# Features of six query groups turned by DMA as two 16-bit planes instead of by TensorE

## The chip, the cores and the metric

The kernel runs on one core of one Trainium2 chip. The metric is the time of one execution in microseconds of device time; smaller is better. A profiled execution also gives a span (from its first to its last recorded instruction) and a trace of every engine: PE (TensorE), DVE (VectorE), ACT (ScalarE), POOL (GpSimd) and SP, whose queue issues nearly all of this kernel's DMAs.

## The reference

Two stages stand behind each other. The first is attention with polynomial features: for each of 4 batches and 4 heads, with 1088 positions and 32 values a head, each row of q and k is projected with S1 and with S2 to 8 values each, and the outer product of the two gives 64 features. The second is a feed-forward layer with a squared ReLU, 128 to 2048 to 128, on all 4352 tokens.

```python
def phi(x):
    a = np.einsum('rd,bhsd->bhsr', S1, x)
    b = np.einsum('rd,bhsd->bhsr', S2, x)
    return np.einsum('bhsi,bhsj->bhsij', a, b).reshape(*x.shape[:-1], r * r)
q_p, k_p = (phi(q), phi(k))
kv = np.einsum('bhsf,bhsd->bhfd', k_p, v)
z = np.sum(k_p, axis=2)
num = np.einsum('bhsf,bhfd->bhsd', q_p, kv)
den = np.einsum('bhsf,bhf->bhs', q_p, z)[..., None] + 1e-06
x = (num / den), heads side by side          # 4352 x 128
out = relu(x @ w_in) ** 2 @ w_out
```

The output is 4352 x 128 in float32.

## The kernel before

**Tiling.** A batch's 1088 positions are 1024, dealt as eight positions to each of 128 partitions, and a remainder of 64. The 1024 are worked as two groups of four tiles of 128 tokens: group (b, g) is half g of batch b, 512 tokens with all four heads. The remainders of two batches share a tile.

**What is done to a group of q.** `turned` (L247, DVE) or, for groups (0, 1) and (3, 1), `proj_t` (L230, PE) brings the 32 values of a head onto partitions. `projected` (L210, PE) projects with S1 and S2, `features` copies the result out of PSUM (L59, ACT) and forms the outer products `ph` (L251, POOL in most groups): 128 tokens by 1024 values, that is 4 tiles with 256 features (4 heads of 64). The features have to lie on partitions for the next product, so `feature_t` (L390) turns them with PE, eight transposes of 128x128 in float32 into two PSUM tiles, and ACT copies each to SBUF (L59, `sb`). `numerators` (L210, `nd`) multiplies them with the batch's k-v sums `kvbd`. `normalize` (L443 to L482, DVE and two small steps of POOL) divides by the denominator and scales each token into 16 bits; the scale is kept in `beta` and multiplied back at the store. Its result `xs` is turned by a DMA transpose from SP (L486) into `xT`, except in three chunks where PE does it.

**What is done to a group of k.** `k_gen` turns, projects and forms features in the same way, and sums them with v (`Kv`, L313, PE). The sums are copied to `kvbd` by DVE (L60). Numerators of batch b need the sums of batch b. From batch 2 on, v is loaded by 32 small DMAs (`load_v`, L110).

**The feed-forward stage** runs over chunks of 512 tokens, one for each group of q (group (0, 0) gives two chunks of 256, and all remainders give one of 256). A chunk is 16 blocks. A block is a first product (`pg`, L708, 16-bit operands, 512 wide), its ReLU (ACT, L715, `gt`), the square (DVE, L716, `g2`) and the second product (`po`, L735, float32), which sums over the 16 blocks in PSUM. `first_product` and `block` keep the first product LOOK = 2 blocks ahead of the second. `pg` has two PSUM buffers, `g2` three SBUF buffers. At the end of a chunk ACT copies the sum (L648), PE turns it back (L652), DVE scales it (L681) and SP stores it (L689). The last chunk (L745) is computed with tokens on partitions already.

**Order.** The first part, up to the first group, is written out by hand (`start`). Behind it the program is recorded in lanes: each generator yields how many blocks are to pass before its next piece, `pump` runs at most two pieces between two blocks, and `drain` empties the lanes. A planner in the compiler then orders each engine's instructions by its own expectation of when operands are ready; what stands in `pinned` stays behind all that was recorded before it on its engine, and so do the loads marked pin and the DMA transposes on SP. At run time every engine and the SP queue work strictly in the order they were given. In batch b the lanes of the first half hold group (b, 1) of q, all of k for batch b+1 and the remainders; those of the second half hold group (b+1, 0) of q. The loads of k and v for batch b+2 are recorded ahead of a batch (ahead of the second half for b = 0) and q's ahead of the second half.

**PSUM and SBUF tiles that the change touches.** `t_ps` shares the two PSUM buffers tagged "ms" with other small tiles; `nd` and the k-v sums share one buffer tagged "nd". `phT0` and `phT1` have two SBUF buffers each.

## Time and profile before

| | |
|---|---|
| median of 3 runs | 210.41 us (210.34 to 210.86) |
| the profiled execution | 210.01 us |
| its span | 208.1 us |
| PE busy | 198.9 us |
| DVE busy | 146.5 us |
| ACT busy | 108.6 us |
| POOL busy | 46.2 us |
| granted TensorE clock | 1.00 |
| bytes moved by DMA | 12.15 MB |

How to read it: the page gives the busy time of each engine, the chain of work that ended last (followed back from the last instruction, at each step to what released it), and groups of instructions by line with the number of times, the busy time in all, the mean time of one in ns, and the idle time of the engine just before them with what ended it. A busy PE is not a PE at its peak, since matmuls are pipelined. Idle time of an engine that is not on the chain costs nothing. Rows of a timeline give start, length, engine, line, operation, destination and source, the number of merged instructions, and in brackets how long the engine stood idle before and who released it.

### The profile page before, as it was taken

What the parts mean: (1) busy time and instruction counts of PE and PEld (TensorE: products, weight loads), DVE (VectorE), ACT (ScalarE), POOL (GpSimd) and SP (SyncE); (2) the same over time, 40 slices, a digit from 0 to 9 for tenths busy, and PEclk for the clock granted to TensorE, in tenths of its full rate; (3) what the DMA queues carried; (4) which work ended last, traced back from release to release, by engine and by line L of the source; (5) the groups of instructions that cost most, each with busy time, mean ns of one, the idle gap of its engine ahead of it and who ended that gap; (6) DMA issues with size and microseconds to landing.
All of it is one profiled execution on the core that took longest, in us unless ns stands there. A gap on an engine that the chain in (4) does not pass through costs nothing.

```text
span 208.1 us, 5407 instructions
## 1 busy us (share of the span) xinstructions
PE 198.9 (96%) x2217; PEld 123.9 (60%) x2217; DVE 146.5 (70%) x281; ACT 108.6 (52%) x206; POOL 46.2 (22%) x66
## 2 busy tenths in 40 slices
PE   7979997999999999999999999999999899999993
PEld 6857885754535553555534556446445454779992
DVE  2869569657787899767776667666968677766662
ACT  3458673265455546356455553555555445555550
POOL 1001346004040863004220951031103110000000
PEclk9999999999999999999999999999999999999999
DMA  6899205222324121402010201010000101010001
GB/s 167 220 339 323 43 3 143 36 31 52 103 67 99 31 35 54 129 1 54 0 27 5 52 3 28 0 36 18 11 14 16 37 3 25 2 50 13 16 0 50
DMA packets 29000, 12.15 MB, mean 58 GB/s; under 512 B 16560, under 2 KB 28592, under 8 KB 28976
## 3 DMA queue, kind: packets, MB, share of 16 engines
q1 hardware_dynamic: 28896, 11.81, 21.8%
q8 instruction: 17, 0.28, 0.6%
q14 instruction: 7, 0.06, 0.1%
q10 hardware_dynamic: 80, 0.01, 0.0%
HBM read 8.79 MB, written 2.23 MB: 53 GB/s over the span
## 4 chain that ended last, share of the span: by engine, by line
PE 88%; DVE 7%; POOL 2%; issue 1%; ACT 1%; DVEq 0%; ACTq 0%
PE po L735 47%; PE pg L708 14%; PE po L745 7%; PE nd L210 4%; PE ab_ps L210 4%; PE t_ps L390 3%; DVE g L716 3%; PE kv_ps L313 3%; PE o_ps L652 2%; PE kv_first L189 1%; PE xt_ps L230 1%; POOL ph L251 1%; PE kv_first L313 1%; DVE xs L473 1%; DVE rtop L453 1%
## 5 line engine op out<-in xcount | busy, mean ns | idle before, releaser
L716 DVE TENSOR_TENSOR g<-gt 128x512 f32<-128x512 f32 x136 | 102.2, 762 | 44.3 <-ACT gt L715 42.7
L735 PE MATMUL po<-g,w_o 128*128 128x512 f32 (+1 forms) x288 | 123.3, 525 | 1.2 <-DVE g L716 1.2
L715 ACT ACTIVATE gt<-pg 128x512 f32<-128x512 f32 x136 | 81.3, 600 | 53.7 <-PE pg L708 52.1
L735 PEld LDWEIGHTS po<-g,w_o 128*128 128x128 f32 x288 | 52.3, 191 | 27.6 <-issue 11.1
L251 POOL TENSOR_TENSOR ph<-ab 128x512 f32<-128x512 f32 (+1 forms) x27 | 31.9, 1204 | 64.8 <-ACT ab L59 64.8
L708 PE MATMUL pg<-xT,w_in 128*128 128x512 f16 x112 | 42.6, 381 | 0.0
L708 PEld LDWEIGHTS <-w_in 128*128 128x128 f16 x160 | 15.3, 98 | 20.4 <-issue 16.8
L479 POOL TENSOR_SCALAR mp<-mm 128x4 f32<-128x4 f32 (+2 forms) x11 | 5.8, 527 | 54.2 <-DVE mm L459 54.2
L745 PEld LDWEIGHTS po<-w_o,g 128*128 128x128 f32 x128 | 16.6, 192 | 0.6
L745 PE MATMUL po<-w_o,g 128*128 128x128 f32 x128 | 16.6, 276 | 0.0
L59 ACT COPY sb<-t_ps 128x512 f32<-128x512 f32 (+1 forms) x18 | 9.2, 515 | 10.4 <-PE t_ps L390 10.4
L59 ACT COPY ab<-ab_ps 128x256 f32<-128x256 f32 (+1 forms) x19 | 6.4, 340 | 15.7 <-PE ab_ps L210 14.1
L210 PEld LDWEIGHTS ab_ps<-w_bd,xt 128*32 128x32 f32 (+1 forms) x476 | 8.9, 114 | 6.9 <-issue 4.2
L210 PE MATMUL ab_ps<-w_bd,xt 128*32 128x64 f32 (+1 forms) x476 | 11.9, 223 | 0.4 <-DVE w_bd L774 0.3
L390 PEld LDWEIGHTS t_ps<-iden,ph 128*128 128x128 f32 x60 | 7.5, 141 | 6.8 <-issue 4.9
L210 PEld LDWEIGHTS nd<-kvbd,sb 128*32 128x32 f32 x480 | 7.9, 110 | 5.4 <-issue 2.6
L210 PE MATMUL nd<-kvbd,sb 128*32 128x66 f32 x480 | 9.6, 222 | 0.0
L390 PE MATMUL t_ps<-iden,ph 128*128 128x128 f32 x60 | 9.4, 274 | 0.0
L59 ACT COPY xt<-xt_ps 128x512 f32<-128x512 f32 (+1 forms) x11 | 5.1, 471 | 5.5 <-PE xt_ps L230 5.4
L708 PE MATMUL pg<-xT_h,w_in 128*128 128x256 f16 x32 | 6.1, 274 | 0.0
L313 PEld LDWEIGHTS kv_ps<-v_main,ph 128*32 128x32 f32 x384 | 3.9, 109 | 3.7 <-POOL beta L482 1.7
L247 DVE STREAM_TRANSPOSE xt<-t 128x512 f32<-128x512 f32 x9 | 6.1, 693 | 0.0
(71 smaller groups left out, 110.5 us busy)
## 6 DMA issues: line engine op xcount, KB each, us to landing
t<-in_k_dram SPq DMA_DIRECT2D x3, 512.0 KB, 3.9
t<-in_q_dram SPq DMA_DIRECT2D x3, 512.0 KB, 4.4
out_dram<-o_sb SPq DMA_DIRECT2D x20, 64.0 KB, 1.7
w_in<-in_moe_w_in_dram SPq DMA_DIRECT2D x2, 512.0 KB, 6.7
w_o<-in_moe_w_out_dram SPq DMA_DIRECT2D x2, 512.0 KB, 7.7
v_turned<-in_v_dram SPq DMA_DIRECT2D x64, 16.0 KB, 1.7
k_sb<-in_k_dram SPq DMA_DIRECT2D x2, 256.0 KB, 3.0
q_sb<-in_q_dram SPq DMA_DIRECT2D x2, 256.0 KB, 4.8
```

Of the source, the lines that this page charges most:

```text
L59: return nc.scalar.copy(dst, src)
L210: nc.tensor.matmul(out_ps[p0 + c : p0 + c + m, c0 : c0 + w], lhsT[:, l0 + c : l0 + c + m], rhs,)
L247: nc.vector.transpose(out=xt[:, :], in_=_v(src, 128 * g, [[NJ * D, 4], [1, 128]]))
L251: eng.tensor_tensor(out=_v(ph, 256 * t0, [[64, 4 * w], [8, 8], [1, 8]]), in0=_v(ab, 64 * t0, [[16, 4 * w], [1, 8], [0, 8]]), in1=_v(ab, 64 ...
L313: nc.tensor.matmul(self.ps[c : c + self.m, at : at + w], _v(ph, c0 + 128 * pr + c, [[1, self.m]], p0, n), v_of(2 * pr + c // 64), start=c ...
L390: nc.tensor.transpose(t_ps[:, 128 * t : 128 * t + 128], ph[:, 256 * t + 128 * pr : 256 * t + 128 * pr + 128], iden[:, :],)
L479: nc.gpsimd.tensor_scalar(out=mp[:, 0:T], in0=mm[:, 0:T], scalar1=1.0 / 1024.0, scalar2=None, op0=mult)
L708: nc.tensor.matmul(pg[:, nt * i : nt * i + nt], w_in[:, 128 * (c + i) : 128 * (c + i) + 128], xT[:, 0:nt],)
L715: last_relu[0] = nc.scalar.activation(gt[:, :], pg[:, :], Relu).ins
L716: nc.vector.tensor_tensor(out=g2[:, :], in0=gt[:, :], in1=gt[:, :], op=mult)
L735: last_product[0] = nc.tensor.matmul(po[0][:, 0:nt], w_o[:, 128 * c : 128 * c + 128], g2[:, nt * i : nt * i + nt], start=(c == 0), stop=(c ...
L745: nc.tensor.matmul(po[t // 2][:, 128 * (t % 2) : 128 * (t % 2) + 128], g2[:, 128 * t : 128 * t + 128], w_o[:, 128 * c : 128 * c + 128], st ...
```

## The change

For the six groups of batches 1 to 3 the features are no longer turned by PE. `features_by_dma` sees the float32 features as pairs of 16-bit halves. ACT copies the low halves into one tile of 128x1024 16-bit elements and the high halves into another (`cut`, four copies of 128x512). SP turns each tile with one DMA transpose into eight blocks of 128x128 (`plane`). ACT then writes the two planes into the low and high halves of `phT` (four copies of 128x512, every second 16-bit element written). The two transposes are pinned in SP's order.

The work is recorded earlier, too. What made a group from turn to numerators in one lane (`q_gen`) is cut in two: `phi_gen` (turn, projection, features, planes) and `x_gen` (numerators, normalization). `phi_gen` of (b+1, 0) and then its `x_gen` are recorded in the first half of batch b, that of (b+1, 1) in the second half of batch b, and `x_gen` of (b, 1) in the first half of batch b. `x_gen` waits in its lane until the batch's k-v sums are done (`summed`), and for (3, 1) until nine chunks exist. The `drain` in the middle of a batch is gone. Group (0, 1) keeps PE's transposes (`second_gen`).

Last, LOOK is 3, and `g2` has four buffers.

```diff
+    def features_by_dma(ph, eng):
+        cut = [apool.tile([128, 1024], U16, name=f"cut{x}", tag=f"cut{x}") for x in range(2)]
+        turned = [apool.tile([128, 1024], U16, name=f"plane{x}", tag=f"plane{x}") for x in range(2)]
+        halves = ph.bitcast(U16)
+        for x in range(2):
+            for y in range(2):
+                eng.copy(
+                    cut[x][:, 512 * y : 512 * y + 512], _v(halves, 1024 * y + x, [[2, 512]])
+                )
+            pinned(nc.sync.dma_start_transpose(
+                _v(turned[x], 0, [[128, 8], [1, 128]]), cut[x][:, :]
+            ))
+            yield 1
+        yield 4
+        phT = [
+            apool.tile([128, 512], F32, name=f"phT_d{pr}", tag=f"phT{pr}") for pr in range(2)
+        ]
+        for x in range(2):
+            for pr in range(2):
+                eng.copy(
+                    _v(phT[pr].bitcast(U16), x, [[256, 4], [2, 128]]),
+                    _v(turned[x], 128 * pr, [[256, 4], [1, 128]]),
+                )
+                yield 1
+            yield 1
+        return phT
...
-    def x_gen(b, g, phT, m=32):
+    def x_gen(b, g, phT=None, m=32):
+        while b not in summed or (b, g) == (B - 1, 1) and len(chunks) < LAST:
+            yield 1
+        if phT is None:
+            phT = phT_of[b, g]
         nd = numerators(b, phT, m)
...
-    def q_gen(b, g, outer, m=32):
+    def phi_gen(b, g, outer):
         eng = nc.scalar
-        if (b, g) == (0, 1):
-            ph = features(ab_second[0], 4, "ph_q", eng, outer)
-        else:
-            xt = proj_t(q_sb[b], g, 4, eng) if (b, g) in BY_PE else turned(q_sb[b], g)
-            yield 1
-            ph = proj(xt, 4, "ph_q", eng, outer, m=m)
+        xt = proj_t(q_sb[b], g, 4, eng) if (b, g) in BY_PE else turned(q_sb[b], g)
+        yield 1
+        ph = proj(xt, 4, "ph_q", eng, outer)
+        yield 3
+        phT_of[b, g] = yield from features_by_dma(ph, eng)
+
+    def second_gen(outer, m):
+        ph = features(ab_second[0], 4, "ph_q", nc.scalar, outer)
         yield 3
         phT = []
         for pr in range(2):
-            phT.append(feature_t(ph, 4, pr, eng))
+            phT.append(feature_t(ph, 4, pr, nc.scalar))
             yield 1
-        yield from x_gen(b, g, phT)
+        yield from x_gen(0, 1, phT)
...
-    LOOK = 2
+    LOOK = 3
...
-        g2 = fpool.tile([128, 512], F32, tag="g2")
+        g2 = fpool.tile([128, 512], F32, tag="g2", bufs=4)
...
-        add_work(second if b == 0 else q_gen(b, 1, (pool,)))
+        add_work(second if b == 0 else x_gen(b, 1))
         if b + 1 < B:
             add_work(k_gen(b + 1, (pool,)), after=6 if b == 0 else 0)
+        if b + 1 < B:
+            add_work(
+                phi_gen(b + 1, 0, (pool,)), x_gen(b + 1, 0), after=7 if b == 0 else 2
+            )
...
-        drain()
...
         if b + 1 < B:
-            add_work(q_gen(b + 1, 0, (pool,)))
+            add_work(phi_gen(b + 1, 1, (pool,)))
```

In the changed file the parting copies are L409, their transposes L412, the joining copies L422, DVE's turn L248, the ReLU L755, the square L756, the second product L775 and the transpose of `xs` L517.

## The prediction

> **What bounds the kernel now.** I read the page first (engine shares, chain that ended last, costliest groups), then the busy time by stretch, then the SP queue in order of time, then one stretch of the timeline. Groups are named (batch, group); an output chunk is 512 tokens of one group.
>
> ```profile
> span 208.1 us, 5407 instructions
> PE 198.9 (96%) x2217; PEld 123.9 (60%) x2217; DVE 146.5 (70%) x281; ACT 108.6 (52%) x206; POOL 46.2 (22%) x66
> ...
> PE 88%; DVE 7%; POOL 2%; issue 1%; ACT 1%; DVEq 0%; ACTq 0%
> ...
> L59 ACT COPY sb<-t_ps 128x512 f32<-128x512 f32 (+1 forms) x18 | 9.2, 515 | 10.4 <-PE t_ps L390 10.4
> ...
> L390 PE MATMUL t_ps<-iden,ph 128*128 128x128 f32 x60 | 9.4, 274 | 0.0
> ```
> PE carries the end; ACT has room in sum. In the chain in order of time a block (second product 0.86, next first product 0.21) repeats every 1.075 us, and four feature transposes (L390) take 0.44.
>
> The busy time by stretch, cut where a chunk's store begins on PE, the first at a chunk's start (length, then busy of PE, PEld, DVE, ACT, POOL):
> ```profile
> 45.00:66.80 21.80, 21.80 (x144) 10.41 (x141) 15.76 (x28) 11.73 (x21) 5.15 (x6) 1.00 0.31 78
> 66.80:91.95 25.15, 24.70 (x384) 13.18 (x383) 21.39 (x41) 12.68 (x25) 9.42 (x11) 1.00 0.23 53
> 91.95:112.46 20.51, 20.51 (x159) 10.17 (x157) 15.23 (x26) 11.29 (x20) 4.89 (x6) 1.00 0.08 21
> 112.46:137.10 24.64, 24.64 (x386) 13.48 (x384) 16.09 (x30) 12.70 (x26) 9.56 (x9) 1.00 0.07 18
> ```
> Sixteen blocks are 17.2 us. With the other PE work of each stretch, by the chain's durations (store transposes 0.44, projections 0.58 a group, numerators 1.07, k-v sums 1.75, feature transposes 0.87), the work is 22.2, 20.2 and 23.4 us in the last three: PE stood still for 2.9, 0.3 and 1.2 us, and by the same count 0.7 and 1.4 in the next two. The reader sees PE busy all the time; the gaps are in the waits. The second stretch shows their cause:
> ```profile
> 68.39 5.04 POOL L251 TENSOR_TENSOR ph<-ab 128x512 f32<-128x512 f32 x4 [8.74 <-ACT ab L59]
> ...
> 71.15 1.35 DVE L716 TENSOR_TENSOR g<-gt 128x512 f32<-128x512 f32 x1
> ...
> 72.42 1.02 DVE L453 TENSOR_TENSOR rtop<-small,small 128x4 f32<-128x4 f32 x1
> ...
> 75.33 1.13 PE L735 MATMUL po<-g,w_o 128*128 128x512 f32 x2 [0.41 <-DVE g L716]
> ```
> While POOL makes features, DVE's squares take 1.2 to 1.5 us instead of 0.69, and PE waits for squares. The SP queue:
> ```profile
> 32.44 0.38 SPq L79 DMA_DIRECT2D t<-in_k_dram  x1
> 32.88 16.94 SPq L110 DMA_DIRECT2D v_turned<-in_v_dram  x32
> 49.91 0.39 SPq L79 DMA_DIRECT2D t<-in_q_dram  x1
> ...
> 60.55 16.59 SPq L110 DMA_DIRECT2D v_turned<-in_v_dram  x32
> ...
> 83.43 1.22 SPq L486 DMA_TRANSPOSE xT<-xs  x1
> ```
> SP is a queue with two plugs of 17 us: the 32 small loads of v. What stands behind one starts late.
>
> **Removed from PE.** Eight transposes a group, 2 x 0.44; six groups: 5.2 us. On ACT 12 copies of 0.585 go (7.0 us). Projections, numerators and the DVE turn stay and only move.
>
> **Added on ACT.** 48 copies of 128x512 16-bit elements, every second one read or written. No row shows such a copy; nearest is the cast from SBUF to 16 bits (L795), 0.635 us, two of which start 0.50 apart when nothing is waited for. Ends: 0.48 apart, as ACT's copies from PSUM follow each other, and 1.0 if skipping halves the rate. I take 0.5, the nearest row. ACT's busy time becomes 108.6 - 7.0 + 48 x 0.6 = 130 us; a ReLU and one copy fit in a block (1.0 of 1.075). What counts is the order: parting waits for POOL, joining for a DMA, and ReLUs stand behind both. With two pg buffers a ReLU has two blocks less its own time, 2.15 - 0.21 - 0.60 - 0.06 = 1.3 us, before PE stops; LOOK = 3 leaves that as it is and gives squares one block (1.075) more.
>
> **Added on SP.** Twelve transposes of 128x1024. The row is half as wide: 1.19 us of SP, landing 2.3 us after issue begins. Ends: 1.2 us if issue is fixed, 2.4 if it doubles. Plain loads of any width cost SP about 0.4, so I take a fixed 0.4 and 0.8 for each 512 columns: 2.0, landing at 3.2. By the Trainium skill (Advanced Engine Details and Errata, X-Bar Transpose) transposing DMAs are as fast as regular ones; by that rule the sum would be the last one under cheap transposes. The row of 1.19 beside 0.38 for a load of four times the bytes contradicts it here.
>
> **The walk down the queues**, in the changed program's instruction order with the durations above.
> - Batch 1's first group. POOL's features of q stand behind one k group and ahead of the other: 28.2 + 2 x 2.54 = 33.3. The four parting copies end at 33.9 and 34.9, with ReLU 14 of the first chunks and the other k group's copy behind them; that group's features end at 37.8 instead of 34.9, still ahead of the PSUM buffer that its sums need (freed by the normalization of (0,1) at 38.9). From there 1.5 of k-v sums, 2.15 of second products and 0.4 of small work bring PE to chunk (0,1) at 43.1, its first ReLU to 43.9. Meanwhile the two transposes hold SP until 38.0, and behind them stands k of batch 2: DVE's turn waits for it, and behind the turn the k-v copy and the squares of (0,1). Issue 38.05, landing 4.0 later at 42.1, turns until 43.4, copy 43.9, square 44.6. Chunk (0,1) starts at 44.8 against 45.0: hidden by PE's own path. A microsecond more here would show.
> - The first plug now runs 38.5 to 55.4 (before: 32.9 to 49.8). Behind it q of batch 2 lands at 59.6 (its traffic before ended 4.1 after issue), and the planes of (1,1) at 60.2 and 61.5. The numerators of (1,0) stand behind second product 10 of the chunk, not 7: 44.8 + 10 blocks + 0.7 + 1.07 = 57.3. Then ACT, which has the first join ahead of ReLU 14, holds it until 60.7; with the joins of the second plane ReLU 16 ends at 63.8. DVE has q's turn ahead of square 13 and the normalization: they start at 60.3, and with squares 14 and 15 between, xs is ready at 64.8. Its transpose finds SP free; xT lands at 67.2, and after product, ReLU and square (1.7) chunk (1,0) starts at 68.9 against 64.9: +4.0, though 1.1 us of its PE work (projection and half the numerators of (1,1)) lies behind it already.
> - Second plug 66.7 to 83.3; then a store, the xT of (1,1) (landing at 86.0, about when its first product is due), planes of (2,0) to 88.95, and q of batch 3, landing at 93.1. DVE's turn of it stands before the squares of chunk (1,1). PE's work of 21.9 us and some DVE waits would let that start at 91 to 92; the turn makes it 94.5 against 90.0: +4.5.
> - No plugs follow. Chunk (1,1): 19.3 of work (17.2, store 0.44, projection 0.58, numerators 1.07) and 0.3 for joins that come 1.5 us late, against 20.5: +3.6. Chunk (2,0): 22.6 and 0.8, as POOL still slows DVE, against 24.6: +2.3. (2,1): 19.7 and 0.5 against 20.5: +2.1 (unrounded). From (3,0) to the end 48.6 before: less 0.87 for transposes, 0.58 for the projection and 0.44 for the turn on PE, all gone or moved ahead, and 1.2 of 1.4 us of waits for DVE, since POOL's features of (3,1) have left this stretch: 45.5. Sum: -1.0.
>
> The end moves from 204.25 to 203.2. The profiled execution took 210.0 (span 208.1, 1.9 around it), so 209.0; the median of the runs shown is 0.4 above it: 209.4. LOOK's worth has its own ends: if it mends no DVE wait the sum is +1.5, if all, -2.5.
>
> **Rivals.**
> *Cheap transposes.* With 1.2 of SP and landing at 2.3 the first plug starts 1.6 us sooner, q of batch 2 lands at 58.0, chunk (1,0) starts at 67.2, q of batch 3 lands at 89.8 and nothing waits for it: +1.3 at (1,1), joins never late, -4.7 in the end: 205.7. For it: the transfer itself keeps the DMA engines busy for some 0.55 us. Against it: issue, not transfer, fills the 1.19. Were issue as short as a plain load's, 0.4, the same walk gives -7: 203, which I give 0.03 of this case's chance, as the narrower row is three times that already.
> *The queue gives it all back (slower).* Transposes that hold SP 2.4 us and land at 4.6, the second behind the first and both behind a 512 KB load. Both plugs and the loads after them come 0.8 to 1.6 us later and the turn of q stops DVE accordingly: +1.6 at the end; each of three later groups adds 1 us of late joins: 213. It decides once a transpose costs SP more than 2.2 us. The Trainium skill's table of rules (VectorE: DVE Perf Modes, Rules for kernel authors) points the same way: transpose on TensorE where PSUM will do. The row agrees as far as the stay goes: 2.3 us by DMA against 0.44 for four on PE.
> *ACT becomes the bound.* At 1.0 us a copy each group adds 8 x 0.5 us, less 2 of slack: four late groups, 217. Against it: strided copies such as ab (L59, 256 elements) cost 0.37, as the plain 128x256 ones.
>
> **Chances.** A measurement here tells 0.3% (0.6 us) from nothing. My forecast 0.42 (range 207.5 to 211.5), cheap 0.18, queue 0.32, ACT 0.08. In the forecast's own case six in ten are faster, a quarter the same. Faster: 0.25 + 0.18 = 0.43; same 0.11; slower 0.06 + 0.32 + 0.08 = 0.46. So the likeliest single case is slightly faster and the signs are even, since slow cases lie further off. The range runs from the cheap case, 205.3, to 214.0, past the queue's 213.
>
> **What would show it.** L390's successor with 12 transposes in place of 60; ACT at 242 instructions, copies at 0.6; the SP rows of the new transposes at 2.0 each; DVE idle before its turn (L248) for loads of q, near 58 to 60 and 92; ACT idle before joins (L422) for DMAs; PE gaps near 61 to 68 and 92 to 94 only; no waits for squares of 0.4 us and more elsewhere. Wrong would be: transposes at 1.2 or 2.4; loads that land elsewhere than 4 us after issue; copies over 0.7; squares still late in chunk (2,0).

## The result

The changed kernel takes 216.22 us (median of 6 runs, 215.37 to 218.34); the kernel before, measured beside it, takes 210.52 (6 runs, 210.34 to 210.86). The ratio is 1.0285, 95% interval 1.0238 to 1.0332: slower by 5.7 us, where a gain of 1.0 us had been forecast, and above the range. Here and below, a ratio leaves out executions that took over 1.5% longer than the fastest of the same kernel, while a median is of all.

The profiled execution took 215.37 us. Its page, in the lines that answer those shown of before (span, busy time, the granted clock over 40 slices, the shares of the chain that ended last, and the two new groups of copies with count, busy time, mean ns, and the idle time before them):

```profile
span 213.6 us, 5352 instructions
PE 198.0 (93%) x2169; PEld 121.0 (57%) x2169; DVE 141.5 (66%) x281; ACT 126.2 (59%) x242; POOL 45.2 (21%) x66
...
PEclk9988999959999999999999999999999999999998
...
PE 68%; POOL 7%; DMA 6%; DVE 5%; ACT 4%; issue 4%; SPq 4%; ACTq 0%; DVEq 0%
...
L422 ACT COPY phT_d<-plane 128x512 uint16<-128x512 uint16 x24 | 18.4, 774 | 4.7 <-DMA plane<-cut 3.5
L409 ACT COPY cut<-ph 128x512 uint16<-128x512 uint16 x24 | 14.2, 621 | 9.7 <-POOL ph L252 9.7
```

PE's share of the chain fell from 88% to 68%: POOL, DMA, ACT, SP's queue and "issue" (time in which an engine waited for nothing that the profile shows) now stand on the path. PE's busy time went down by only 0.9 us, although 48 transposes are gone (some 5 us by the chain's durations). The likely reason is that for some stretches its clock was halved: PE was busy for 8.4 us in three windows of half clock, where work takes about twice as long (an estimate of 4.2 us more). The PEclk line was full throughout before.

Where the time was lost shows when each chunk's first second product starts (us from the trace; the last column is the end of the span):

| kernel | first | (0,1) | (1,0) | (1,1) | (2,0) | (2,1) | (3,0) | end |
|---|---|---|---|---|---|---|---|---|
| before | 17.2 | 45.0 | 64.7 | 89.9 | 110.4 | 135.0 | 155.5 | 208.1 |
| after | 18.4 | 51.5 | 73.3 | 99.1 | 118.9 | 144.2 | 164.4 | 213.6 |
| later: | +1.2 | +6.5 | +8.6 | +9.2 | +8.5 | +9.2 | +8.9 | +5.5 |

The first column differs by up to 1.2 us among the profiled kernels of this study, so it is better to compare stretches. From the first product to chunk (0,1): 27.8 us before, 33.1 after, +5.3. The next two stretches: +2.1 and +0.6. From (1,1) to the end 118.2 before, 114.5 after: -3.7. The changed program gains late, though less than the 5.5 us that the prediction had from (1,1) on (+4.5 there, -1.0 at the end), and loses more than that at the start.

The busy time by stretch (cut as before; length, PE, PEld, DVE, ACT, POOL, granted clock, DMA share, GB/s):

```profile
51.48:75.83 24.35, 23.87 (x224) 11.14 (x224) 17.03 (x33) 18.44 (x36) 5.32 (x7) 1.00 0.36 88
75.83:101.00 25.17, 22.79 (x312) 11.15 (x311) 18.58 (x38) 15.17 (x31) 8.87 (x11) 1.00 0.37 76
101.00:121.96 20.96, 20.93 (x214) 10.31 (x212) 15.41 (x30) 14.33 (x26) 4.47 (x6) 1.00 0.20 46
121.96:146.80 24.84, 23.29 (x318) 12.17 (x317) 14.74 (x25) 16.24 (x33) 8.76 (x9) 1.00 0.21 39
```

The SP queue after (start, length, operation, number of merged DMAs):

```profile
35.28 2.69 SPq L412 DMA_TRANSPOSE plane<-cut  x2
38.06 0.54 SPq L80 DMA_DIRECT2D t<-in_k_dram  x1
38.65 16.64 SPq L111 DMA_DIRECT2D v_turned<-in_v_dram  x32
55.39 0.39 SPq L80 DMA_DIRECT2D t<-in_q_dram  x1
...
71.17 16.91 SPq L111 DMA_DIRECT2D v_turned<-in_v_dram  x32
```

Two transposes hold SP for 2.7 us, so 1.2 to 1.3 each, and the first plug (the 32 loads of v) begins 5.8 us later than before, ending at 55.3. That is close to where the prediction had it (38.5 to 55.4), so SP is not where the time beyond the forecast came from.

It came from 33 to 49 us. The timeline of the changed kernel there (start, length, engine, line, operation; in brackets how long the engine stood idle before and who released it):

```profile
29.55 5.04 POOL L252 TENSOR_TENSOR ph<-ab 128x512 f32<-128x512 f32 x4 [5.36 <-ACT ab L60]
33.15 0.62 ACT L409 COPY cut<-ph 128x512 uint16<-128x512 uint16 x1 [0.95 <-POOL ph L252]
34.63 1.66 ACT L409 COPY cut<-ph 128x512 uint16<-128x512 uint16 x3 [0.86 <-POOL ph L252]
36.20 0.36 ACT L60 COPY ab<-ab_ps 128x256 f32<-128x256 f32 x1
36.46 0.60 ACT L755 ACTIVATE gt<-pg 128x512 f32<-128x512 f32 x1
...
40.32 0.67 DVE L504 TENSOR_TENSOR xs<-nd,small 128x512 f16<-128x512 f32 x1
41.14 1.63 PE L314 MATMUL kv_ps<-v_main,ph 128*32 128x33 f32 x124 [2.14 <-DVE xs L504]
44.57 0.33 PE L314 MATMUL kv_ps<-v_main,ph 128*32 128x33 f32 x4 [1.79 <-issue]
```

The same place in the kernel before:

```profile
35.52 0.69 DVE L473 TENSOR_TENSOR xs<-nd,small 128x512 f16<-128x512 f32 x1
36.36 0.76 PE L313 MATMUL kv_ps<-v_main,ph 128*32 128x33 f32 x64 [1.37 <-POOL ph L251]
37.17 1.03 PE L735 MATMUL po<-g,w_o 128*128 128x256 f32 x4
38.12 0.77 PE L313 MATMUL kv_ps<-v_main,ph 128*32 128x33 f32 x64
40.01 0.43 PE L313 MATMUL kv_ps<-v_rem,ph 64*32 64x64 f32 x16
```

Three things stand behind each other here. (1) ACT stands before the parting copies until POOL has q's features; the other k copy (36.20) and ReLUs wait behind them, the squares behind those, and on DVE the normalization that frees the PSUM buffer of the k-v sums ends at 41.0 (before: 36.2). PE is idle for 2.14 us. (2) PE then runs 124 matmul records of the sums without a break, where second products stood between two halves of 64 before, and stops for 1.79 us with nothing to wait for that the profile shows. (3) In two windows of 3.41 us PE has half its clock:

```profile
38.30:41.71 3.41, 1.27 (x69) 0.90 (x71) 3.30 (x5) 0.00 (x0) 1.26 (x3) 1.00 0.81 217
41.71:45.13 3.42, 1.63 (x87) 1.41 (x74) 1.31 (x2) 0.00 (x0) 0.00 (x0) 0.50 0.26 40
45.13:48.54 3.41, 3.41 (x24) 2.05 (x24) 0.45 (x2) 0.00 (x0) 0.00 (x0) 0.50 0.21 33
```

In the last one PE is busy all the time and does what takes about half as long elsewhere: the 16 matmuls of the v remainder took 0.65 us for 0.43, four second-product records 2.07 for 1.03.

### The profile page after: what moved, and what is told of

It reads as the page before. It is cut to its first block, busy times and chain, and to the rows that moved or that the text cites. A ratio compares the mean times of both kernels' runs of the same rounds, so it can differ in the third digit from the quotient of the medians.

```text
span 213.6 us, 5352 instructions
## 1 busy us (share of the span) xinstructions
PE 198.0 (93%) x2169; PEld 121.0 (57%) x2169; DVE 141.5 (66%) x281; ACT 126.2 (59%) x242; POOL 45.2 (21%) x66
## 4 chain that ended last, share of the span: by engine, by line
PE 68%; POOL 7%; DMA 6%; DVE 5%; ACT 4%; issue 4%; SPq 4%; ACTq 0%; DVEq 0%
PE po L775 38%; PE pg L748 12%; POOL ph L252 7%; PE po L785 7%; PE nd L211 3%; DMA w_in<-in_moe_w_in_dram 3%; DVE g L756 3%; PE ab_ps L211 2%; PE kv_ps L314 2%; DMA plane<-cut 2%; ACT gt L755 2%; SPq L80 1%; SPq L95 1%; DMA v_turned<-in_v_dram 1%; SPq L111 1%
## 5 line engine op out<-in xcount | busy, mean ns | idle before, releaser
L756 DVE TENSOR_TENSOR g<-gt 128x512 f32<-128x512 f32 x136 | 99.6, 745 | 53.6 <-ACT gt L755 53.1
L775 PE MATMUL po<-g,w_o 128*128 128x512 f32 (+1 forms) x288 | 124.3, 529 | 0.0
L755 ACT ACTIVATE gt<-pg 128x512 f32<-128x512 f32 x136 | 80.6, 601 | 33.1 <-PE pg L748 31.8
L775 PEld LDWEIGHTS po<-g,w_o 128*128 128x128 f32 x288 | 53.5, 194 | 26.1 <-DVE g L756 8.5
L422 ACT COPY phT_d<-plane 128x512 uint16<-128x512 uint16 x24 | 18.4, 774 | 4.7 <-DMA plane<-cut 3.5
L409 ACT COPY cut<-ph 128x512 uint16<-128x512 uint16 x24 | 14.2, 621 | 9.7 <-POOL ph L252 9.7
L510 POOL TENSOR_SCALAR mp<-mm 128x4 f32<-128x4 f32 (+2 forms) x11 | 4.0, 366 | 72.5 <-DVE mm L490 72.5
L211 PEld LDWEIGHTS nd<-kvbd,phT_d 128*32 128x32 f32 x384 | 6.0, 110 | 5.2 <-issue 3.3
L314 PE MATMUL kv_ps<-v_main,ph 128*32 128x33 f32 x384 | 5.0, 206 | 3.9 <-DVE xs L504 2.1
L211 PE MATMUL nd<-kvbd,phT_d 128*32 128x66 f32 x384 | 7.3, 223 | 0.0
L689 ACT COPY oT<-po 128x512 f32<-128x512 f32 (+1 forms) x9 | 4.7, 518 | 3.6 <-PE po L775 3.6
```

The source lines that it names most:

```text
L211: nc.tensor.matmul(out_ps[p0 + c : p0 + c + m, c0 : c0 + w], lhsT[:, l0 + c : l0 + c + m], rhs,)
L314: nc.tensor.matmul(self.ps[c : c + self.m, at : at + w], _v(ph, c0 + 128 * pr + c, [[1, self.m]], p0, n), v_of(2 * pr + c // 64), start=c ...
L409: eng.copy(cut[x][:, 512 * y : 512 * y + 512], _v(halves, 1024 * y + x, [[2, 512]]))
L422: eng.copy(_v(phT[pr].bitcast(U16), x, [[256, 4], [2, 128]]), _v(turned[x], 128 * pr, [[256, 4], [1, 128]]),)
L689: nc.scalar.copy(oT[:, 0:nt], po[:, 0:nt])
L755: last_relu[0] = nc.scalar.activation(gt[:, :], pg[:, :], Relu).ins
```

## The experiments

Each kernel is measured beside the kernel before on the same chip; intervals are 95%. Starts of chunks are from one profiled execution of each.

### LOOK alone

The kernel before with one part of the change only.

```diff
-    LOOK = 2
+    LOOK = 3
...
-        g2 = fpool.tile([128, 512], F32, tag="g2")
+        g2 = fpool.tile([128, 512], F32, tag="g2", bufs=4)
```

> The kernel before with LOOK = 3 and four buffers of g2, nothing else. If the extra block only helps the squares (my theory): 207.5 to 210, with the half-clock stretches absent. If the deeper look is what costs the changed kernel its time: 212 or more, with a gap near 39 us.

208.6 us (208.49 to 208.73), ratio 0.9889 [0.9865, 0.9912]. PE's waits for squares fall from 6.6 us (longest 1.5) to 3.0 (longest 0.3), and the full clock stays. So this part gains some 2.3 us and is no cause of the loss; the planes and the move must cost 7 to 8 us on top.

### The change without LOOK

The same two lines undone in the changed kernel.

```diff
-    LOOK = 3
+    LOOK = 2
...
-        g2 = fpool.tile([128, 512], F32, tag="g2", bufs=4)
+        g2 = fpool.tile([128, 512], F32, tag="g2")
```

> The changed kernel with LOOK = 2 and three buffers of g2. If the loss is made by parting copies that hold ACT (my theory): no better, 216 to 219, with the gap and the half clock near 40 us still there. If LOOK is to blame: 210 to 212.

219.54 us (218.36 to 221.12), ratio 1.0412 [1.0357, 1.0467]. The gap, the pause and the half clock at 40 to 51 us are there as well. LOOK is worth some 3 us here (3.3 by the medians, 2.7 by the ratios); whether that is more than alone, the intervals don't tell.

### The first group late

The planes of (1,0) and its numerators are recorded in the second half of batch 0, where before had that group; everything else as in the changed kernel.

```diff
-        if b + 1 < B:
+        if 0 < b < B - 1:
             add_work(
-                phi_gen(b + 1, 0, (pool,)), x_gen(b + 1, 0), after=7 if b == 0 else 2
+                phi_gen(b + 1, 0, (pool,)), x_gen(b + 1, 0), after=2
             )
...
-        if b + 1 < B:
+        if b == 0:
+            add_work(phi_gen(1, 0, (pool,)), x_gen(1, 0), phi_gen(1, 1, (pool,)))
+        elif b + 1 < B:
             add_work(phi_gen(b + 1, 1, (pool,)))
```

> The changed kernel with planes and numerators of group (1,0) recorded in the second half of batch 0, ahead of those of (1,1). The first half has no parting copies and no transposes. By both theories of the first half (ACT held by POOL; SP held by the transposes) chunk (0,1) starts near 45 to 46 us at full clock; but the planes of (1,0) now stand behind the loads of v, so chunk (1,0) starts late: 211 to 214 in all.

215.04 us (214.44 to 215.69), ratio 1.0194 [1.0162, 1.0227]. Chunk (0,1) starts at 45.7, as early as before. So the loss at that place belongs to the moved group. But the group now has its planes behind the first run of v loads, and chunk (1,0) starts at 74.1: the stretch between is 28.5 us against 19.7. The loss has changed places, with idle PE and a half clock (69.3 to 76.1 us) there.

### Parting copies behind their ReLU

The planner had put each parting copy ahead of ReLUs that were recorded earlier and were ready. Here it may not.

```diff
+                with tc.issue_after(last_relu[0]):
                     eng.copy(
                         cut[x][:, 512 * y : 512 * y + 512], _v(halves, 1024 * y + x, [[2, 512]])
                     )
```

> The changed kernel with each parting copy put behind the ReLU recorded just before it on ACT; the transposes' place in SP's queue is unchanged. If ACT held by POOL makes the loss: the ReLUs and the normalization of (0,1) are on time, k-v sums start near 37 to 39, no half clock there, 210 to 213 in all. If SP is to blame (k of batch 2 behind the transposes): the transposes come later still, DVE waits longer for k, and the time is 216 or more.

213.6 us (212.91 to 214.89), ratio 1.014 [1.0089, 1.019]. The normalization ends at 38.7 instead of 41.0 and the sums start sooner, but chunk (0,1) still starts at 50.9:

```profile
36.77 2.17 ACT L410 COPY cut<-ph 128x512 uint16<-128x512 uint16 x4
...
38.82 1.41 PE L314 MATMUL kv_ps<-v_main,ph 128*32 128x33 f32 x124 [1.27 <-DVE xs L506]
42.52 0.32 PE L314 MATMUL kv_ps<-v_main,ph 128*32 128x33 f32 x4 [2.29 <-issue]
```

What was gained ahead of the sums was lost behind their start: from there to chunk (0,1) it takes 12.1 us against 10.3. 0.5 us of that is a longer pause; the rest fits the half clock (41.5 to 48.4 us), which now falls on more of PE's work, but was not measured apart. The first cause is real and does not stand alone.

### The sums split

The second half of batch 1's k-v sums is recorded one block later and behind a second product, so that 64 matmul records stand in a row where 128 stood.

```diff
         for g in range(2):
-            kv.tiles(phs[g], g, range(4))
-            yield 1
+            with ExitStack() as behind:
+                if b == 1 and g == 1:
+                    behind.enter_context(tc.issue_after(last_product[0]))
+                kv.tiles(phs[g], g, range(4))
+            yield 2 if b == 1 and g == 0 else 1
```

> The changed kernel with the second group's half of batch 1's k-v sums recorded one block later and behind a second product, so that 64 small matmuls stand in a row on PE where 128 stood. Theory (the start of chunk (0,1) comes late for three reasons behind each other: normalization late behind ACT's parting copies, then PE without instructions at the end of the 128 small matmuls, then a TensorE clock of 0.5): the pause of 1.79 us on nothing visible goes, PE gains 1.5 to 2 us there, and if the clock falls because of that pause it stays at 1.0: 213 to 214.5. If the clock falls for the 2.1 us of idle time before the sums alone, a window of 0.5 near 41 to 48 stays: 214.5 to 215.5. Rival (the pause is a wait for data that the trace names badly): the pause stays in another place, 216. Rival (all of the loss is on SP's queue): no change, 216.

214.2 us (213.21 to 215.11), ratio 1.0143 [1.0092, 1.0195]. Chunk (0,1) starts at 48.6, 2.9 us sooner. The pause did not go, it is 1.40 us, behind record 58 of the second half. Counted from the start of the program it stands behind the 599th matmul record of PE, and so it does in every kernel of this study that pauses there, whatever that record is. The idle time before the sums is the same 2.14 us as in the changed kernel, yet the clock stays full at this place in this execution; it falls at 84.5 to 87.9 instead:

```profile
40.12:43.53 3.41, 2.03 (x124) 1.57 (x125) 2.43 (x4) 0.00 (x0) 0.00 (x0) 1.00 0.55 145
81.08:84.50 3.42, 1.45 (x14) 0.51 (x12) 1.51 (x6) 2.12 (x5) 2.29 (x3) 1.00 0.21 33
84.50:87.91 3.41, 3.41 (x73) 1.75 (x69) 3.27 (x9) 1.83 (x5) 1.02 (x3) 0.50 0.47 130
```

### Both

The last two edits in one kernel.

> Both edits together: parting copies behind the ReLU recorded before them, and the k-v sums of batch 1 split by a second product. Parting copies alone gave 213.6 us, with a pause of 2.29 us inside the sums and a clock of 0.5 from 41.5 to 48.4. Theory: both gone, chunk (0,1) starts at about 47 instead of 51, 210 to 211.5, level with the kernel before. Theory with the clock hanging on the idle time before the sums alone: 212. Rival (late loads behind the transposes on SP hold the chunk): chunk (0,1) still starts near 51 and 213.6 stays.

209.87 us (five runs, 209.12 to 213.17), ratio 0.9946 [0.9895, 0.9996]. The profiled execution, 209.12, has the full clock throughout. The mean granted clock of the five falls as their time grows: 1.00 at 209.1 and 209.2 us, 0.992 at 209.9, 0.984 at 211.6 and 0.976 at 213.2. One window of 3.41 us at half clock lowers the mean over 208 us by 0.008, so these are, by estimate, none, one, two and three such windows. Its k-v sums:

```profile
38.33 0.75 PE L314 MATMUL kv_ps<-v_main,ph 128*32 128x33 f32 x64 [1.27 <-DVE xs L509]
39.02 0.70 PE L780 MATMUL po<-g,w_o 128*128 128x256 f32 x2
39.65 0.71 PE L314 MATMUL kv_ps<-v_main,ph 128*32 128x33 f32 x58
42.03 0.26 PE L314 MATMUL kv_ps<-v_main,ph 128*32 128x33 f32 x6 [1.67 <-issue]
```

Chunk (0,1) starts at 46.4. Two edits of the order, which take away neither the planes nor their transposes nor LOOK, take back 6.3 of the 6.8 us between forecast and result. Alone they gave 2.6 and 2.0, and in the profile of each the clock still fell in one place. By the ratios, which set each kernel against the kernel before on its own chip, it is 7.1 us together and 3.0 for each alone.

### PE kept busy with zeros

Six matmuls of zeros, accumulated into the second product, are placed ahead of batch 1's k-v sums in the changed kernel.

```diff
+        if b == 1:
+            with tc.issue_after(last_product[0]):
+                for _ in range(6):
+                    nc.tensor.matmul(
+                        po[0][:, 0:256], zero[:, 0:128], zero[:, 0:256],
+                        start=False, stop=False, skip_group_check=True,
+                    )
         kv = Kv(b)
```

> The changed kernel with six matmuls of zeros, added to the running sum of the second product (they add nothing), placed on PE ahead of batch 1's k-v sums where PE stands idle for 2.1 us; the compiler's planner then also puts second products between the two halves of the sums. Leaves nothing out, adds about 3 us of PE work. Theory (idle time and the pause are what lower the clock): the clock stays 1.0 through 41 to 49, no pause, chunk (0,1) starts 1.5 to 3 us earlier although PE does more: 213.5 to 214.5. Rival (the lower clock has another source, such as power at that time): a window of 0.5 stays and the extra work costs up to 1 us: 216 to 217.

215.66 us (215.01 to 216.66), ratio 1.0218 [1.0178, 1.0257]: less than expected. Chunk (0,1) starts at 50.1 with 3 us more work on PE and the clock full at 41 to 49 us. But the zeros were done before the gap (2.01 us idle remained), the pause is there (1.16 us, again behind record 599, now record 50 of the second half), and the clock falls later, at 87.4 to 90.8. So the experiment did not price the half clock alone. One of its four executions had a mean granted clock of 1.00 and took 215.5 us, in the midst of the other three (215.0 to 216.7 at 0.992), so here a fall of the clock cost nothing that can be seen. What it does show is that the pause keeps its place in the count of matmul records: with the zeros ahead it came behind 114 records of the sums instead of 124, and again behind record 599.

### The pause without planes

The kernel before with LOOK = 3, and batch 1's sums recorded in one piece, one block later.

```diff
         kv = Kv(b)
+        if b == 1:
+            yield 1
         for g in range(2):
-            kv.tiles(phs[g], g, range(4))
-            yield 1
+            with ExitStack() as behind:
+                if b == 1:
+                    behind.enter_context(tc.issue_after(last_product[0]))
+                kv.tiles(phs[g], g, range(4))
+            if b > 1 or g:
+                yield 1
```

> No planes at all: the kernel before with LOOK = 3 (208.6 us), and batch 1's k-v sums recorded in one piece, one block later, so that 128 matmul records stand in a row on PE as they do in the changed kernel. Theory (PE ran out of fetched instructions behind the 599th matmul record of the program, in all six kernels that paused; where second products lay in the run of small matmuls PE was slow enough for the fetch): a pause of 1 to 2.5 us behind record 599, without any data to wait for, and perhaps a lower clock behind it: 209.5 to 211. Rival (the pause belongs to the planes, their DMAs or their waits): no pause, 208.3 to 209.

208.12 us (207.94 to 208.71), ratio 0.988 [0.9863, 0.9898]: no time lost, against the expectation, and level with LOOK alone. There is a pause, behind matmul record 600, and a short one:

```profile
37.35 1.41 PE L313 MATMUL kv_ps<-v_main,ph 128*32 128x33 f32 x128 [0.40 <-POOL ph L251]
...
40.27 0.60 PE L741 MATMUL po<-g,w_o 128*128 128x256 f32 x2
41.38 0.70 PE L741 MATMUL po<-g,w_o 128*128 128x256 f32 x2 [0.51 <-issue]
```

Here the 128 small records end at 38.8 and second products follow before the place is reached; in the changed kernel the run of small records ended just at it. So a pause at this place needs no planes. That its length depends on how little time PE needs for the instructions ahead of it fits these two kernels and is not shown: the pause of 1 to 2.5 us that was expected here did not come.

### Planes from batch 2 on

Batch 1 goes back to PE's transposes in the places of before; the four groups of batches 2 and 3 keep the planes, with the parting copies behind their ReLU.

```diff
-        phT_of[b, g] = yield from features_by_dma(ph, eng)
+        if b == 1:
+            phT = []
+            for pr in range(2):
+                phT.append(feature_t(ph, 4, pr, eng))
+                yield 1
+            phT_of[b, g] = phT
+        else:
+            phT_of[b, g] = yield from features_by_dma(ph, eng)
...
-        add_work(second if b == 0 else x_gen(b, 1))
+        if b == 1:
+            add_work(phi_gen(1, 1, (pool,)), x_gen(1, 1))
+        else:
+            add_work(second if b == 0 else x_gen(b, 1))
...
-        if b + 1 < B:
+        if 0 < b < B - 1:
             add_work(
-                phi_gen(b + 1, 0, (pool,)), x_gen(b + 1, 0), after=7 if b == 0 else 2
+                phi_gen(b + 1, 0, (pool,)), x_gen(b + 1, 0), after=2
             )
...
+        if b == 0:
+            drain()
...
-        if b + 1 < B:
+        if b == 0:
+            add_work(phi_gen(1, 0, (pool,)), x_gen(1, 0))
+        elif b + 1 < B:
             add_work(phi_gen(b + 1, 1, (pool,)))
```

> Batch 1 goes back to PE's transposes in the old places of the lanes (with the drain in the middle of batch 0); the planes remain for the four groups of batches 2 and 3, with the parting copies behind the ReLU recorded before them; LOOK is 3 as in the changed kernel. Theory (the loss is made where batch 1's first group is moved into the first chunks and where its planes meet the first run of v loads; from batch 2 on planes gain): starts as with LOOK alone up to chunk (1,1), 90.4 us, then stretches of 20.0, 23.6 to 25.4, 20.0, 19.3 and 29.7: span 203 to 205, time 205 to 206.5, below both kernels and below LOOK alone (208.6). Rival (the planes cost ACT and SP as much as PE gains anywhere): 208 to 210. Rival (the loss is SP's second run of loads with planes behind it): chunk (2,0) starts later than 112, 209 or more.

207.97 us (207.66 to 208.68), ratio 0.9857 [0.9821, 0.9894]. That misses the 205 to 206.5 of the theory and lies next to its rival's 208 to 210. Up to chunk (1,0) it runs as LOOK alone (45.8, 65.6), and from (1,1) on its stretches are 19.8, 23.6, 19.9, 19.3 us against 20.4, 24.6, 20.4, 21.3; to the end it takes 4 us less than LOOK alone. But from (1,0) to (1,1) it takes 27.7 us against 24.6, with ACT standing before the first join of (2,0) with ReLUs behind it:

```profile
85.85 3.43 SPq L414 DMA_TRANSPOSE plane<-cut  x2
...
89.24 1.38 ACT L424 COPY phT_d<-plane 128x512 uint16<-128x512 uint16 x2 [3.04 <-DMA plane<-cut]
...
92.06 0.38 PE L757 MATMUL pg<-xT,w_in 128*128 128x512 f16 x1 [2.06 <-ACT gt L764]
```

### Joins later, three times

First in the changed kernel with both edits, then in the kernel with planes from batch 2 on: the joins are recorded eight blocks behind the transposes instead of four, each behind the ReLU recorded before it.

```diff
-        yield 4
+        yield 8
         phT = [
...
+                with tc.issue_after(last_relu[0]):
                     eng.copy(
                         _v(phT[pr].bitcast(U16), x, [[256, 4], [2, 128]]),
```

> As with both edits before (parting copies behind their ReLU, batch 1's sums split: 209.9 us), and the joining copies recorded eight blocks behind the transposes instead of four, each behind the ReLU recorded before it. Theory (what is left of the planes' price is ACT standing before joins for planes that have not landed, up to 3 us at one place near 86 to 89, with ReLUs behind): that wait goes, chunks (1,0) to (2,0) start 1 to 3 us sooner: 207 to 209. Rival (the loads of q behind the 17 us runs of v loads hold DVE, as the prediction had it): chunk (1,0) and (1,1) start where they did, 209.5 to 210. Rival (joins behind ReLUs make numerators late): 211 or more.

212.36 us (10 runs, 209.69 to 214.35), ratio 1.0028 [0.999, 1.0066], the worst of what was expected. The joins of (1,0) now stand behind the parting copies of (1,1), and the stretch from (0,1) to (1,0) grows from 22.1 to 25.4 us; from there to the end it takes 2.6 us less. Much of the scatter goes with the clock: the three executions at 0.997 and more took 209.7 to 211.1 us, the five at 0.991 and 0.992 took 212.1 to 213.2, the two at 0.984 took 213.7 and 214.4. At the full clock that is 0.6 to 2 us more than both edits without late joins (209.1); the rest of the 212.36 goes with the falls of the clock.

> The kernel with planes for batches 2 and 3 alone (207.97 us, in which ACT stood 3.04 us before the first join of (2,0), with ReLUs behind it, and chunk (1,1) started at 93.4 instead of 90.4), and its joins eight blocks behind the transposes, each behind the ReLU recorded before it. Theory: the 3 us come back, chunk (1,1) starts at 90.5, time 204.5 to 206. Rival (something else than the join holds that place, such as k-v sums): 207.5 to 208.5.

209.17 us (208.75 to 212.4), ratio 0.9918 [0.9898, 0.9938], above what was expected. In the profiled execution, at 212.4 the longest of five (the others took 208.8 to 209.5, so it overstates the loss), chunk (1,1) starts at 91.4 instead of 93.4, near the 90.5 expected, but (2,0) at 117.8 instead of 113.1. The four joins of (2,0) run there from 98.0 to 104.7, with the parting copies of (2,1) between them. ACT does not stand idle before those parting copies, so that they held the joins by waiting for POOL, as the next expectation says, is not shown.

With the joins behind their ReLU, but four blocks behind the transposes as in the changed kernel, they stand behind the first ReLUs of chunk (1,1) and ahead of those parting copies (the diff above without its first two lines):

> Planes for batches 2 and 3 alone, each join behind the ReLU recorded before it, and recorded four blocks behind the transposes as in the changed kernel, so that the joins of (2,0) stand behind the first ReLUs of chunk (1,1) but ahead of the parting copies of (2,1). Theory (ACT's strict order decides: a join or a parting copy that waits holds the ReLUs and the other copies behind it; eight blocks were too late since the joins then stood behind parting copies that wait for POOL): no wait of 3 us before the first join of (2,0), chunk (1,1) starts near 91, chunk (2,0) near 111, 205.5 to 207. Rival (joins behind ReLUs make numerators late as such): chunk (2,0) starts at 114 or later, 208.5 to 210. Rival (no difference from the order of joins): 208.

206.64 us (205.79 to 207.01), ratio 0.9794 [0.9754, 0.9833]. The joins of (2,0) run from 92.0 to 99.1, chunk (1,1) starts at 91.0, (2,0) at 112.2. This kernel beats the one before by 2.1% and LOOK alone (0.9889) by some 2 us; its page has

```profile
span 204.9 us, 5369 instructions
PE 196.0 (96%) x2185; PEld 120.5 (59%) x2185; DVE 144.4 (70%) x281; ACT 120.6 (59%) x230; POOL 47.1 (23%) x66
...
PEclk9999999999999999999999999999999999999999
```

## Why the prediction was wrong

**What was removed and added** came as counted. ACT has 242 instructions and PE 48 fewer. The parting copies take 0.62 us, as costed; the joins 0.77, over the 0.7 that was named as a sign of error. That is 24 x 0.17 = 4 us of ACT more than at the 0.6 taken, with ACT still at 59%. The transposes hold SP 1.24 us (median; 1.23 to 1.34) and land after 2.7: nearly the cheap end, where 2.0 and 3.2 had been taken. The issue of a transposing DMA hardly grows with its width (1.19 for 128x512). The 1.19 that the prediction set against a load's 0.38 is SP's time to issue and doesn't bear on the speed of the transfer: from issue to landing the narrow transposes, of 128 KB, took 2.3 us, plain stores of 128 KB 1.9 and 2.9.

**The step that failed is "Batch 1's first group ... hidden by PE's own path".** It said that chunk (0,1) would start at 44.8 against 45.0; it started at 51.5. Its pieces, forecast and measured:

| | forecast | after |
|---|---|---|
| POOL's features of q done | 33.3 | 34.6 |
| last parting copy ends | 34.9 | 36.3 |
| k's other features done | 37.8 | 39.2 |
| normalization of (0,1) frees the buffer | 38.9 | 41.0 |
| k-v sums begin to end, remainder included | 1.5 | 5.5 |
| first ReLU of chunk (0,1) done | 43.9 | 50.7 |

The whole is 6.8 us late, and its parts add up as follows. 1.2 us is the later start of this execution (18.4 against 17.2; the clock was at half from 14.4 to 17.8), which no part of the change explains. 0.9 us is the normalization. The walk had ReLU 14 and the k copy behind the parting copies, as it was, and took them to be covered; but the normalization stands on DVE behind squares of those ReLUs, and DVE is slower while POOL makes features (a step of the normalization on 16 elements took 1.03 us at 38.2, beside them, and 0.16 in the kernel with parting copies behind, where it came after them). "A microsecond more here would show" was right. 4.0 us is the row of the sums, costed by the chain at 1.5 and measured at 5.5: 1.8 is the pause, 1.2 a second product at half clock that fell between (the forecast had counted it behind the sums), and 0.65 the remainder's matmuls, also at half clock, which the forecast may have had in its 0.4 of small work. 0.6 us is the way from there to the chunk, at half clock for its first part. Neither the pause nor a clock below 1.00 was in any step.

How these divide is read from the two edits. From the start of the sums to chunk (0,1) the changed kernel needed 10.3 us; with the sums split, and the full clock there, 7.8. The pause accounts for 0.4 of these 2.6 us, which leaves some 2 us for the clock, by this reckoning. Parting copies behind their ReLUs bring the sums forward by 1.7 us, counted from the first second product. With both the kernel takes 209.9 us, against a forecast of 209.4.

**The rest of the walk** held in sum, and that is partly luck. From chunk (0,1) to the end it had 158.4 us (44.8 to 203.2). Its end lay 3.9 us ahead of the end of the span (204.25 of 208.1); taken off the measured 162.1 and 160.9 us, that leaves 158.2 in the changed kernel and 157.0 with both edits. Two misses cancel in it: from (0,1) to (1,1) the walk had 49.7 us and 47.6 were measured, from (1,1) to its end it had 108.7 and 110.7 were measured. The mechanism differs, too. The loads of q were named as what makes (1,0) and (1,1) late, and in the changed kernel DVE's turn never waits for them; the only such wait is 0.8 us, for k. What waits is ACT: 9.7 us before parting copies (longest 3.1, at 85.4, with PE idle for 1.97 us behind it) and 3.5 us before joins. The walk costed late joins in batches 2 and 3 at 0.3 us and parting copies behind POOL, past the first group, at nothing. With the planes of batches 2 and 3 alone, the order of joins moves the end by 2.5 us (209.2 against 206.6). This is probably also why the nearly cheap transposes did not bring the cheap rival's 205.7, together with the loss at the first group: what SP gave, ACT's order took. That was not tested apart.

**The rivals.** "ACT becomes the bound" came closest in time (217), and that is luck: its copies of 1.0 us took 0.62 and 0.77, and ACT had room in sum. It lost time by its strict order. "The queue gives it all back" (213) needed more than 2.2 us a transpose and is refuted. That PE itself would pause and slow down was not among the rivals.

**LOOK** was given ends of +1.5 and -2.5 on the sum. Alone it is worth 2.3 us. In the changed kernel PE's waits for squares are 8.5 us (longest 0.6), more than the 6.6 before, probably since late ReLUs make late squares.

**Two readings in the working** were wrong, and set no step of the forecast, since (1,1) was set by DVE's turn. The stretch from 66.80 was given 22.2 us of PE work and the one from 112.46 23.4, but the trace has the same 128 + 16 records of k-v sums, 72 of numerators and 104 of projections in both, and 8 against 10 feature transposes; so PE stood still for some 1.9 us in the first, and not for 2.9. And the range began at 205.3, which was called the cheap case, while that case's own sum is 205.7.

What stays open is the price of the half clock. No edit changed it alone, and its 2 us are worked out from two profiles. Executions of one and the same kernel tell a little more: the kernel before took 211.5 to 211.8 us in the four executions with a mean clock of 0.990 or 0.991 and mostly 210.5 to 211.1 in the others, which is some 0.9 us for one window; with both edits it was 0.7 us for the first window and 2.4 for two, in the kernel with late joins some 2 us for one, in the kernel with zeros nothing. Idle time may make both the lower clock and the longer time, so these differences are not a price either. The changed kernel had at least two such windows in all six executions (0.959 to 0.984).

## What to carry to other kernels

When a copy that waits for a slow engine or a DMA is added to an engine that works strictly in order, ask at each place what the planner puts behind it; totals of busy time (59% here) say nothing about that. Keep the parting and joining work of a new path out of the stretch in which PE already stands still, and look there for what a further microsecond sets off. Before giving up on a change that lost as a whole, try it stage by stage: with four of the six groups, and two orders fixed, the kernel ran 4.2 us below the one before, some 2 of them from the planes and the rest from LOOK.

## What the runs showed of the hardware

**The TensorE clock and idle time.** All edges of the half-clock windows of an execution lie on a grid of 3.41 us. I took PE's busy share in each window of that grid, between 10 and 200 us of the profiles of all 14 kernels. Eight windows at full clock, in eight kernels, had a share of 0.20 to 0.45 and were followed by half clock; windows with 0.52 and more were followed by the full clock. There is one exception in either direction: 0.42 without a fall (the kernel with parting copies behind, at 92.7), and 0.61 with one (the changed kernel, at 11.0). Once low, shares of 0.47 to 0.74 kept the clock low for another window, and 0.90 and more raised it but for one. So 1.9 us of idle time within one window were enough, and whether a gap of 2 us does it depends on where the grid cuts it: the 2.14 us of the changed kernel lay in one window, the same 2.14 us with the sums split lay in two (shares 0.55 and 0.59). The Trainium skill (TensorE: Matmul & The Clock Gate, Part 1) has the window, 3413 ns and free-running, and the runs agree; its rule of thumb there (HAM oscillation) that idle gaps beyond some 3.4 us are what throttles is too lenient by these rows, where 2.14 us of gap went ahead of the fall. The grid lay differently against the start of the program in each profile (its first edge at 4.0 to 6.9 us), which would fit the scatter (LOOK alone 0.3 us between its runs, the changed kernel 3.0). The runs without a profile show only their mean clock: 0.998 to 1.00 for LOOK alone, 0.959 to 0.984 for the changed kernel.

**A pause at a fixed place of PE's program.** Behind matmul record 599, in all seven kernels that make the planes of (1,0) early, PE stops for 1.2 to 2.3 us without waiting for data. In each of them a packet of 16 KB of the instruction queue runs just before, and PE goes on 1.3 to 1.5 us after that packet ends (in the changed kernel the packet runs from 42.2 to 43.2, PE goes on at 44.6). From the packet's start to PE's going on it is 2.3 to 2.6 us in all seven, and 2.6 without planes (behind record 600, in the kernel with the sums in one piece). In the six kernels that show no pause PE comes to the place 2.9 us or more after the packet's start (in before the packet starts at 37.6 and the 600th record at 40.75). I read it as PE running out of fetched instructions. The order of the two, the time between them and the fixed place are shown; that the packet holds PE's instructions is inferred.

**Joining copies.** Writing every second 16-bit element costs ACT 0.77 us for 128x512, reading every second one 0.62.
